# Scores over all 64 rows of a half, with zeros in the unused rows, and the right-hand pools 32 bytes lower

## The chip, the cores and the metric

The kernel runs on one core of a Trainium2 chip. The metric is the device time of one execution in microseconds (us). Before the change three runs gave 1689.62, 1690.02 and 1690.09 us; their median is 1690.02 us.

## The reference

Two mixers of the same 2048 x 512 input (batch 1) are blended by a gate. Everything is float32.

```python
g = sigmoid((x * gate_w).sum(-1, keepdims=True))
# A: Fourier mixing, as matrix products
a = einsum("bsd,ed->bse", x, dft_hid_re);  b = einsum("bsd,ed->bse", x, dft_hid_im)
y = einsum("ts,bse->bte", dft_seq_re, a) - einsum("ts,bse->bte", dft_seq_im, b)
# B: softmax attention, 32 heads of width 16, all 2048 keys for all 2048 queries
q, k, v = split(x @ wqkv)
p = softmax(einsum("bhqd,bhkd->bhqk", q, k) * 16 ** -0.5)
o = einsum("bhqk,bhkd->bhqd", p, v) @ wo
out = g * y + (1 - g) * o
```

The attention weights are drawn 64 times larger than usual, so that the softmax needs a maximum taken off its scores.

## The kernel before

**Precision.** Float32 operands are split into a high and a low part (`hi_lo`, lines 83 to 85: ScalarE copies the high part, VectorE or GpSimd subtracts), and a product is made of three matmuls: high by high, high by low, low by high. For queries and keys the three products are stacked along the contraction instead. A *stack* (`qs`, `ks`, lines 198 to 199) is a tile of 128 partitions by 2048 columns for one pair of heads. Head 0 of the pair has partitions 0 to 63 (a *half*), head 1 has partitions 64 to 127. In each half 48 rows hold the three 16-row parts (`load_stacks`, lines 201 to 210), and rows 48 and 49 hold, in `qs`, the negative row maxima in two parts (`m_rows`, lines 239 to 246) and, in `ks`, ones (line 259). Rows 50 to 63 of a half are not used. There are two buffers of each stack, used in turn by the 16 head pairs.

**Stages.** 1. The projections of queries and keys (lines 171 to 193), to about 95 us. 2. The projection of the values: eight row tiles with 128-row matmuls (line 333), then two groups of four tiles (`four`, lines 304 to 327, matmul at line 315) in which two 64-row matmuls, one in each half of the array, run side by side. `four` also runs the first maxima between its matmuls. 3. The imaginary hidden transform, also with `four`. 4. The main part from about 195 us to about 1,640 us: attention for 16 head pairs, woven with the Fourier transforms. 5. The last output projections.

**The main part.** `segment` (line 888) issues slots from a written pattern such as `FULL`. In a slot a matmul of the transforms (`d`, line 416, 64 rows) goes to one half of the array, and a score (`s`, line 721, 50 rows) or a tile for the row maxima (`a`, line 222, 48 rows) goes to the other half. ScalarE takes the exponential of each score tile from PSUM into `pt` (line 722); VectorE takes the maximum of each `a` tile (line 224). At the bar of a pattern the products with the values (line 757) run: they read `pt` and use all 128 rows. Seven PSUM banks are handed out by a small model of when their readers are done (`bank`, `read_by`); a matmul that gets a bank waits for the reader of its last contents.

**The order around the change.** `st1` is a pool on the right side of the on-chip memory; it holds the tile name `hl` with two buffers. The first `hl` tile is `ones`. Its eight DMAs into `ks`, on GpSimd's queue (line 259), wait until the memory of the first stage is free. The first 12 stack loads (lines 209 and 210) and the four loads of `wo` (line 261 with `staged`, line 104) go through SyncE's queue. Then PE computes the values; `v_done` (line 274) copies half of each result with ScalarE (line 277) and half with VectorE (line 278). At row tiles 6, 8, 10 and 12 `v_done` also splits one quarter of `wo` into a new `hl` tile, so ScalarE gets a cast (line 84) at that place of its queue. A new `hl` tile has to wait for whatever still reads the buffer it takes. In the kernel before, tile 6 takes the second buffer, which nobody has used; tile 8 takes the buffer of `ones`. The value tiles go through four PSUM banks in turn, so tile 11 needs the bank of tile 7.

In the built program the right-hand tiles begin at a multiple of 64 bytes plus 32; `pt`, for example, begins at byte 172,448 of each partition. `xab`, `vt`, `qs`, `ks` and the split weights `wv`, `wre`, `ch`, `cl` are on the left, at multiples of 64.

Of the kernel before, what the change touches and what calls it, by code (L numbers as in the profile page):

```python
# [9 lines left out]
F32 = mybir.dt.float32  # L10
# [5 lines left out]
P = 128  # L16
S = 2048
D = 512
# [13 lines left out]
def mix_kernel(ctx: ExitStack, tc: tile.TileContext, xa_t, xa, wqkv, w_hid, w_seq, wo, gate_w, out):  # L32
# [5 lines left out]
    nc = tc.nc  # L38
# [54 lines left out]
    st1 = right.__enter__()  # L93
# [8 lines left out]
    def staged(src):  # L102
        raw = st1.tile([P, D], F32, name="raw", bufs=RAW)
        nc.sync.dma_start(raw, src)
        return raw
# [92 lines left out]
    qs = [main.tile([P, S], F32R, name=f"qs{i}", tag=f"qs{i}") for i in range(2)]  # L198
    ks = [main.tile([P, S], F32R, name=f"ks{i}", tag=f"ks{i}") for i in range(2)]

    def load_stacks(p):
        q_t, k_t = qs[p % 2], ks[p % 2]
        for h in range(2):
            rows = slice((2 * p + h) * DH, (2 * p + h + 1) * DH)
            o = 64 * h

            for i, (qv, kv) in enumerate(((0, 0), (0, 1), (1, 0))):
                part = slice(o + 16 * i, o + 16 * i + 16)
                nc.sync.dma_start(q_t[part].bitcast(F32), qk_d[0][qv, rows])
                nc.sync.dma_start(k_t[part].bitcast(F32), qk_d[1][kv, rows])  # L210
# [41 lines left out]

    ones = st1.tile([2, 2 * D], F32, name="hl", bufs=2)
    nc.gpsimd.memset(ones, 1.0)
    nc.gpsimd.memset(vt[:, :, :, 16:17], 1.0)
    for i in range(2):
        for h in range(2):
            for tb in range(2):
                nc.gpsimd.dma_start(ks[i][64 * h + 48:64 * h + 50, tb * 2 * D:(tb + 1) * 2 * D].bitcast(F32), ones)
    load_stacks(0)  # L260
    wos = [staged(wo[:, kt]) for kt in range(KT)]
    wrs = []
# [87 lines left out]
    work = ctx.enter_context(tc.tile_pool(name="work", bufs=1, side="right", reuse_waits="tile"))  # L350
# [30 lines left out]
    def bank(i=None):  # L381

        nonlocal now
        if i is None:
            i = min(range(7), key=lambda j: free[j])
        now = max(now, free[i] + 0.7)
        return i, banks[i].tile([P, 512], F32, name="t")

    def read_by(i, kind):

        nonlocal dve, act
        if kind == "a":
            dve = max(now + 2.0, dve) + 2.6
            free[i] = dve + 0.4
        else:
            act = max(now + 2.0, act) + 2.1
            free[i] = act + 0.5
# [7 lines left out]
    class Chain:  # L405


        def __init__(self, take, n):
            self.take, self.left = take, n
            self.begun = False  # L410
# [226 lines left out]
    class LastPair:  # L637


        def __init__(self, blk, acc):  # L640
            self.blk, self.acc = blk, acc
            self.oe = work.tile([P, 512], F32, name="oe", bufs=2)
            self.on = work.tile([P, 4, 2, DH], F32, name="on15", bufs=2)
            self.rc = work.tile([P, 4, 2], F32, name="rc15", bufs=2)
            self.o15 = work.tile([P, 2, P], F32R, name="o15", bufs=2)

        def copy(self, n):
            for c in range(n):
                cols = slice(c * 512 // n, (c + 1) * 512 // n)
                nc.scalar.copy(self.oe[:, cols], self.acc[:, cols])  # L650
# [56 lines left out]
    def scores(u, qb, h, ps=None):  # L707
        p, r = divmod(u, 32)
        hf, kt = divmod(r, 16)
        q0 = hf * 1024 + qb * 512  # L710
        if u >= UNITS - 16:

            blk, kt = divmod(kt, 8)
            q0, kt = 1024 + blk * 512, 2 * kt + qb
        if u not in pts:
            pts[u] = work.tile([P, 4, 512], F32, name="pt", bufs=4)
        if ps is None:
            i, ps = bank()
            read_by(i, "s")
        rr = slice(64 * h, 64 * h + 50)  # L720
        nc.tensor.matmul(ps, ks[p % 2][rr, kt * P:(kt + 1) * P], qs[p % 2][rr, q0:q0 + 512], start=True, stop=True)  # L721
        return nc.scalar.activation(pts[u][:, 2 * qb + h], ps, AF.Exp, bias=0.0, scale=DH ** -0.5)  # L722

# [144 lines left out]
    def score(kind, h):  # L868
        x = next(streams[h][kind == "a"], None)
        if x:  # L870
            if kind == "a":
                i, ps = bank()
                read_by(i, "a")
                users.append((kind, a_tile(*x, ps)))
            else:
                users.append((kind, scores(*x)))
# [65 lines left out]
    def first_tiles(phase, j):  # L942

        if j == 3:
            return scores(*next(streams[0][0]), turn_of("a"))
        a_tile(*next(streams[0][1]))
# [17 lines left out]
    for u in range(valued + 2, UNITS, 2):  # L964
        add_sums()
        run_plan(u)
        for i in range(4):
            if i == 2:
                pump(*whole[u])
                if u == 506:  # L970
                    last_pairs[0].turn()
                elif u == 508:
                    last_pairs[0].back()
            for h in range(2):
                scores(u + i // 2, i % 2, h)
            for h in range(2):
                score("a", h)
        if u == 510:
            last_pairs[0].products(())
        values()  # L980
        if deferred:
            deferred.pop(0)()
# [39 lines left out]
```

## Time and profile before

| | us |
|---|---|
| median of three runs | 1690.02 |
| profiled execution, its own time | 1689.9 |
| its span | 1688.1 |
| PE busy | 1676.5 |
| DVE busy | 1371.2 |
| ACT busy | 1246.1 |
| POOL busy | 747.3 |

PE is TensorE's matmuls, PEld its weight loads, DVE VectorE, ACT ScalarE, POOL GpSimd, and SP (SyncE) issues most DMAs. An engine's name with a q is its instruction queue. A row of groups gives line, engine, operation, output<-inputs by the program's names, shapes, count, busy time, mean duration and the idle time before. A row of the timeline gives the start in us from the span's start, the duration, the engine, what it does, and in brackets how long the engine was idle before and what ended that. The ends of matmuls are modelled, so the distance between the starts of two matmuls says more than their durations.

### The profile page before, as it was taken

To read this page: it belongs to the slowest core of one execution; us is meant where nothing else is said; L and a number is where in the kernel's file an instruction comes from. 1 tells how busy PE (TensorE), PEld (TensorE's weight loads), DVE (VectorE), ACT (ScalarE), POOL (GpSimd) and SP (SyncE) were. 2 spreads that over 40 slices of the span, in tenths; PEclk is the share of its full clock that TensorE was granted. 3 is DMA by queue.
4 is the path that set the end of the run, shared out by engine and by line. 5 is a ranking of instruction groups with operands and counts; after the bars stand their busy time and mean duration, and the time that the engine had idled before them with its cause. 6 is when DMAs were issued, how large, how long until landed. Compare 5 with 4: busy or idle time off the path is not lost.

```text
span 1688.1 us, 34488 instructions
## 1 busy us (share of the span) xinstructions
PE 1676.5 (99%) x13072; PEld 1089.9 (65%) x13072; DVE 1371.2 (81%) x2283; ACT 1246.1 (74%) x2472; POOL 747.3 (44%) x807
## 2 busy tenths in 40 slices
PE   9999999999999999999999999999999999999998
PEld 7888766666666666666666666666666666665643
DVE  5448688888888888888888888888888888899944
ACT  5212288887777888777777788778777888787896
POOL 0214634554444465444444466445554465322230
PEclk9999999999999999999999999999999999999999
DMA  9963500314141533314155543332241536640114
GB/s 289 345 153 112 175 11 20 45 51 77 45 83 46 96 102 84 70 46 95 45 133 189 103 121 85 86 67 61 70 89 46 112 94 131 263 70 8 32 29 139
DMA packets 82485, 165.15 MB, mean 98 GB/s; under 512 B 19776, under 2 KB 20032, under 8 KB 78480
## 3 DMA queue, kind: packets, MB, share of 16 engines
q1 hardware_dynamic: 77968, 162.56, 37.1%
q8 instruction: 103, 1.69, 0.4%
q0 software_dynamic: 4352, 0.39, 0.3%
q14 instruction: 62, 0.51, 0.1%
HBM read 107.73 MB, written 54.52 MB: 96 GB/s over the span
## 4 chain that ended last, share of the span: by engine, by line
PE 98%; POOL 1%; issue 0%; DVE 0%; DMA 0%; ACT 0%; DVEq 0%; POOLq 0%; ACTq 0%
PE d L416 40%; PE t L757 27%; PE t L222 10%; PE t L721 9%; PE t L315 4%; PE t L89 2%; PE t L88 2%; PE t L90 2%; PE t L333 1%; PE t L738 1%; PE t L416 0%; PE t L159 0%; POOL hl L292 0%; PE t L675 0%; DMA b<-hl 0%
## 5 line engine op out<-in xcount | busy, mean ns | idle before, releaser
L224 DVE TENSOR_REDUCE mx<-t 128x1 f32<-128x512 f32 x2022 | 1254.3, 684 | 198.7 <-PE t L222 165.4
L722 ACT ACTIVATE pt<-t 128x512 f32<-128x512 f32 x2048 | 1034.6, 631 | 9.5 <-PE t L721 9.3
L721 PE MATMUL t<-qs,ks 50*128 50x512 f32 x2048 | 740.2, 413 | 0.5 <-ACT y L432 0.5
L222 PE MATMUL t<-ks,qs 48*128 48x512 f32 x2022 | 689.8, 400 | 0.0
L416 PE MATMUL d<-xab,ch 64*128 64x512 f32 x2016 | 644.8, 394 | 0.0
L757 PE MATMUL t<-pt,vt 128*32 128x512 f32 x3968 | 477.5, 598 | 0.0
L416 PEld LDWEIGHTS d<-xab,ch 64*128 64x128 f32 x2016 | 366.7, 184 | 133.3 <-issue 92.2
L222 PEld LDWEIGHTS t<-ks,qs 48*128 48x128 f32 x2022 | 366.5, 186 | 62.4 <-DVE mx L224 27.4
L416 PE MATMUL d<-xab,cl 64*128 64x512 f32 x1008 | 397.9, 395 | 0.0
L721 PEld LDWEIGHTS t<-qs,ks 50*128 50x128 f32 x2048 | 366.9, 185 | 33.5 <-ACT pt L722 13.1
L772 POOL TENSOR_TENSOR osum<-osum,oe 128x512 f32<-128x512 f32 x217 | 279.8, 1290 | 168.2 <-ACT oe L766 161.0
L766 ACT COPY oe<-t 128x512 f32<-128x512 f32 x217 | 127.7, 589 | 238.0 <-PE t L757 235.6
L757 PEld LDWEIGHTS t<-pt,vt 128*32 128x32 f32 x3968 | 105.0, 109 | 227.8 <-issue 148.8
L371 POOL CAST ch<-craw 128x512 fp32r<-128x512 f32 x126 | 77.4, 614 | 347.7 <-PE t L721 278.8
L416 PEld LDWEIGHTS d<-xab,cl 64*128 64x128 f32 x1008 | 185.6, 184 | 68.2 <-issue 51.1
L372 POOL TENSOR_TENSOR cl<-craw,ch 128x512 fp32r<-128x512 f32 x126 | 162.3, 1288 | 10.2
L245 POOL DMA_DIRECT2D qs<-mt x128 | 72.3, 570 | 82.5 <-DVE mt L241 75.9
L416 PE MATMUL d<-wo_hl,o_hl 64*128 64x512 f32 (+1 forms) x270 | 72.6, 393 | 0.8 <-DVE yp_qs L596 0.8
L416 PE MATMUL d<-wre,xab 64*128 64x512 f32 x288 | 70.4, 389 | 0.0
L416 PEld LDWEIGHTS d<-wre,xab 64*128 64x128 f32 x288 | 52.9, 185 | 3.9 <-DVE mx L224 0.3
L416 PEld LDWEIGHTS d<-wo_hl,o_hl 64*128 64x128 f32 (+1 forms) x270 | 49.6, 185 | 4.6 <-DVE yp_qs L596 1.3
L89 PE MATMUL t<-xab,wh 128*128 128x512 f32 x128 | 50.2, 392 | 0.0
(121 smaller groups left out, 895.6 us busy)
## 6 DMA issues: line engine op xcount, KB each, us to landing
craw<-w_seq SPq DMA_DIRECT2D x128, 256.0 KB
qk<-hl SPq DMA_DIRECT2D x32, 512.0 KB
qs<-qk SPq DMA_DIRECT2D x96, 128.0 KB
ks<-qk SPq DMA_DIRECT2D x96, 128.0 KB
b<-hl SPq DMA_DIRECT2D x16, 512.0 KB
xab<-b SPq DMA_DIRECT2D x16, 512.0 KB
o<-osum SPq DMA_DIRECT2D x62, 128.0 KB
oh<-nh SPq DMA_DIRECT2D x12, 512.0 KB
```

What stands on the lines that cost most here:

```text
L89: nc.tensor.matmul(ps, sh, ml, start=False, stop=False)
L222: nc.tensor.matmul(ps, qs[p % 2][r, qt * P:(qt + 1) * P], ks[p % 2][r, kb * 512:(kb + 1) * 512], start=True, stop=True)
L224: user = nc.vector.tensor_reduce(mx[p % 2][:, h, qt, kb:kb + 1], ps, AX.X, ALU.max)
L245: (nc.sync, nc.gpsimd)[h].dma_start(rows.rearrange("v (q b c) -> v b q c", q=8, b=4)[:, b], mt[hf][32 * b + h:32 * b + 32:2])
L371: nc.gpsimd.tensor_copy(h1, raw)
L372: nc.gpsimd.tensor_tensor(l1, raw, h1.bitcast(F32), ALU.subtract)
L416: i = nc.tensor.matmul(self.ps, st[r], mv[r], start=not self.begun, stop=stop)
L721: nc.tensor.matmul(ps, ks[p % 2][rr, kt * P:(kt + 1) * P], qs[p % 2][rr, q0:q0 + 512], start=True, stop=True)
L722: return nc.scalar.activation(pts[u][:, 2 * qb + h], ps, AF.Exp, bias=0.0, scale=DH ** -0.5)
L757: nc.tensor.matmul(acc[32 * j:32 * j + 32], vt[:, kt, p, h:h + 32], pt[:, j], start=u == us[0], stop=u == us[-1])
L766: nc.scalar.copy(oe, acc)
L772: nc.gpsimd.tensor_tensor(o, o, oe, ALU.add)
```

## The change

A second `hl` tile, `zeros`, of 14 partitions by 1024 columns is set to zero by GpSimd. Sixteen more DMAs on GpSimd's queue copy it into rows 50 to 63 of each half of both `ks` and both `qs` buffers; they stand between the eight DMAs of the ones. `zeros` takes the second buffer of `hl`, so the split of `wo` at row tile 6 takes the buffer of `ones`, and the one at row tile 8 that of `zeros`. The score matmul reads 64 rows of each operand where it read 50. The added terms are zero times zero. The matmuls of the maxima keep their 48 rows.

A `pad` tile of 8 float32 columns is allocated in each of the two right-hand pools and never written or read. It puts the tiles of these pools 32 bytes lower; they then begin at multiples of 64 bytes (`pt` at 172,416).

The order of the instructions on PE, DVE, ACT and SP is the same as before. On POOL there are one memset and 16 DMAs more. GpSimd's DMAs use eight semaphores in turn, so with 24 in a row each from the ninth on waits for the landing of the one eight places before. The cast of `wo` at row tile 6 on ScalarE waits for the last of the DMAs of the ones, which is now the 22nd of 24; in the kernel before it waited for no such DMA.

```diff
     ones = st1.tile([2, 2 * D], F32, name="hl", bufs=2)
     nc.gpsimd.memset(ones, 1.0)
+    zeros = st1.tile([14, 2 * D], F32, name="hl", bufs=2)
+    nc.gpsimd.memset(zeros, 0.0)
     nc.gpsimd.memset(vt[:, :, :, 16:17], 1.0)
     for i in range(2):
         for h in range(2):
             for tb in range(2):
                 nc.gpsimd.dma_start(ks[i][64 * h + 48:64 * h + 50, tb * 2 * D:(tb + 1) * 2 * D].bitcast(F32), ones)
+                for t in (ks[i], qs[i]):
+                    nc.gpsimd.dma_start(t[64 * h + 50:64 * h + 64, tb * 2 * D:(tb + 1) * 2 * D].bitcast(F32), zeros)
+    st1.tile([P, 8], F32, name="pad")
     load_stacks(0)
...
             self.o15 = work.tile([P, 2, P], F32R, name="o15", bufs=2)
+            if not blk:
+                work.tile([P, 8], F32, name="pad")
...
-        rr = slice(64 * h, 64 * h + 50)
+        rr = slice(64 * h, 64 * h + 64)
         nc.tensor.matmul(ps, ks[p % 2][rr, kt * P:(kt + 1) * P], qs[p % 2][rr, q0:q0 + 512], start=True, stop=True)
```

## The prediction

> **What bounds the kernel now.** I read the page first, then the timeline of the first 130 us and of one segment of the main part, then the single lines that the change touches. The page:
>
> ```profile
> span 1688.1 us, 34488 instructions
> PE 1676.5 (99%) x13072; PEld 1089.9 (65%) x13072; DVE 1371.2 (81%) x2283; ACT 1246.1 (74%) x2472; POOL 747.3 (44%) x807
> PE 98%; POOL 1%; issue 0%; DVE 0%; DMA 0%; ACT 0%; DVEq 0%; POOLq 0%; ACTq 0%
> L224 DVE TENSOR_REDUCE mx<-t 128x1 f32<-128x512 f32 x2022 | 1254.3, 684 | 198.7 <-PE t L222 165.4
> ...
> L721 PE MATMUL t<-qs,ks 50*128 50x512 f32 x2048 | 740.2, 413 | 0.5 <-ACT y L432 0.5
> ```
>
> PE is busy 99% of the span and the chain that ended last is PE for 98% of it. So a pause of PE anywhere is paid in full, and a shorter matmul is gained unless something next to it already waits. The 413 ns of a score look long, but a busy PE is a modelled overlap; distances between starts decide. Here is one segment of the main part:
>
> ```profile
> 703.30 0.50 PE L416 MATMUL d<-xab,ch 64*128 64x512 f32 x1
> ...
> 703.64 0.39 PE L416 MATMUL d<-xab,cl 64*128 64x512 f32 x1
> ...
> 703.65 0.39 PE L222 MATMUL t<-ks,qs 48*128 48x512 f32 x1
> ...
> 704.08 5.00 DVE L224 TENSOR_REDUCE mx<-t 128x1 f32<-128x512 f32 x8 [0.81 <-PE t L222]
> ...
> 705.76 0.40 PE L721 MATMUL t<-qs,ks 50*128 50x512 f32 x1
> 705.76 0.19 PEld L222 LDWEIGHTS t<-ks,qs 48*128 48x128 f32 x1
> ...
> 706.00 0.40 PE L222 MATMUL t<-ks,qs 48*128 48x512 f32 x1
> 706.14 0.18 PEld L721 LDWEIGHTS t<-qs,ks 50*128 50x128 f32 x1
> ...
> 706.74 0.18 PEld L721 LDWEIGHTS t<-qs,ks 50*128 50x128 f32 x1
> 706.84 0.39 PE L416 MATMUL d<-xab,ch 64*128 64x512 f32 x1
> 706.95 0.40 PE L721 MATMUL t<-qs,ks 50*128 50x512 f32 x1
> 707.27 1.92 PE L757 MATMUL t<-pt,vt 128*32 128x512 f32 x16
> ...
> 709.13 0.50 PE L416 MATMUL d<-xab,ch 64*128 64x512 f32 x1
> ```
>
> From the second slot to the sixteenth are 14 steps. The half with the 64-row transforms takes 706.84 - 703.64 = 3.20 us, 0.2286 a step; the half with scores and maxima 706.95 - 703.65 = 3.30 us, 0.2357 a step. The value products follow the slower half. VectorE is close behind: its eight maxima of the segment start when the first `a` tile is done, and one takes (5.00 - 0.68) / 7 = 0.617 us (0.68 being the duration of one, 684 ns in the groups). The third ends near 705.99 and the fourth near 706.61. A weight load normally starts with the matmul before it on its half (705.76 and 705.76); those at 706.14 and 706.74 start late, each 0.13 to 0.15 us after a maximum should be done. So near the segment's end the scores wait for VectorE to free a bank.
>
> **Part 1: 64 rows instead of 50.** 2048 matmuls and 2048 weight loads change their rows; none is added. One bound is no gain at all: 48 and 50 rows go at one pace here, so a row more or less need not count. The other is that each score falls to the transforms' pace: 0.2357 - 0.2286 = 7.1 ns, times 2048 = 14.5 us. A loss is excluded by the transforms, which have 64 rows and are not slower. I take 1 us of gain. The reason is VectorE: its chain begins with the first `a` of the segment and then runs without a pause, and the late weight loads hang on its third and fourth maxima. Scores that come earlier would wait there; only what lies after that point (about one score a segment) and before the first `a` is left, a few ns in each of some 250 segments.
>
> The Trainium skill, page "TensorE: Matmul & The Clock Gate", section "Part 2: What happens when you issue a matmul", says that the time of a weight load goes by its columns and that the number of rows doesn't matter. By that rule this part gives 0 and the sum below would be 1 us higher; the 7.1 ns between the halves would then be due to waits and semaphores, which the scores have and most transforms have not.
>
> **Part 2: 32 bytes lower.** It touches `pt`, `osum`, `oe`, `y` and the staging tiles. Rows with the moving operand on the right (`wch`, off the 64-byte grid before) and on the left (`wv`, on it):
>
> ```profile
> L315 PE MATMUL t<-wch,xab x256: 388/392/399, 141.7 to 193.8; 64*128 64x512 f32 x128
> ...
> L315 PE MATMUL t<-wv,xab x192: 386/390/493, 115.8 to 141.5; 64*128 64x512 f32 x192
> ```
>
> The medians are 392 and 390 ns. If 2 ns were the price of the old place, the value products (16 in a segment, four side by side, so four steps) would gain 4 x 2 x 250 = 2 us; the rest of the traffic is not on the path. Bounds -2 to +2 us; I take 0, since 2 ns lies inside the spread of either row.
>
> **Part 3: sixteen more DMAs on GpSimd's queue.** This is where I expect the time to change. The place, before:
>
> ```profile
> 100.21 4.31 POOL L259 DMA_DIRECT2D ks<-hl  x8 [5.49 <-DMA qk<-hl]
> ...
> 106.06 5.06 SPq L104 DMA_DIRECT2D raw<-wo  x4
> ...
> 115.75 1.20 PE L315 MATMUL t<-wv,xab 64*128 64x512 f32 x8
> 115.99 0.62 ACT L84 CAST hl<-raw 128x512 fp32r<-128x512 f32 x1 [2.46 <-DMA raw<-wo]
> 116.52 0.38 ACT L277 COPY vt<-t 128x256 f32<-128x256 f32 x1
> ...
> 116.80 0.39 PE L222 MATMUL t<-ks,qs 48*128 48x512 f32 x2
> ...
> 116.94 0.42 DVE L278 COPY vt<-t 128x256 f32<-128x256 f32 x1 [2.94 <-ACT vt L277]
> ...
> 118.40 1.77 PE L315 MATMUL t<-wv,xab 64*128 64x512 f32 x14
> ```
>
> The cast at 115.99 is the split of `wo` at row tile 6. After the change it waits for the 22nd of the 24 DMAs. Queued behind it on ScalarE is the copy of value tile 7 (116.52), behind that VectorE's half (ends 117.36), and behind VectorE's copy the maxima. PE needs tile 7's bank when `four` starts its second phase. Of the last row's 14 matmuls six belong to the first phase, so that start is 118.40 + 3 x 0.23 = 119.09 (a step of the row being (1.77 - 0.39) / 6 = 0.23). The slack is 119.09 - 117.36 = 1.7 us. From the cast's start to the end of VectorE's copy are 1.37 us.
>
> When does the 22nd land?
>
> ```profile
> L259 POOL DMA_DIRECT2D ks<-hl x8: 521/521/689, 100.2 to 104.0; - x8
> ...
> DMA to landing us min/median/max: 5.2/8.9/11.3
> ```
> ```profile
> qs<-mt POOLq DMA_DIRECT2D x128, 2.0 KB, 1.7
> ```
> ```profile
> 95.00:116.00 21.00, 21.00 (x94) 17.14 (x95) 3.99 (x10) 2.70 (x8) 4.31 (x8) 1.00 0.91 149
> 116.00:130.00 14.00, 14.00 (x124) 11.43 (x124) 11.35 (x20) 3.19 (x8) 2.62 (x3) 1.00 0.28 100
> ```
>
> The eight issues are 0.54 us apart (100.2 to 104.0). The first lands 5.2 us after its issue, at 105.4, the last 11.3 us after, at 115.3: one each 1.41 us, because the DMA engines are 91% busy with the stack loads until 116. Early bound: at the pace of the issue, with the 1.7 us of a quiet GpSimd DMA, number 22 lands at 100.2 + 21 x 0.54 + 1.7 = 113.2, ahead of 115.99, and nothing is lost. Late bound: at 1.41 us each, 105.4 + 21 x 1.41 = 135.0. Between them: each new DMA brings 14 rows of 4 KB, 57 KB, together 0.92 MB; at the 149 GB/s of that stretch they take 6.2 us, so that the busy time which ended at 116 ends some 4 us later, near 120, when 105.4 + 10 x 1.41 = 119.5 has seen eleven landings. The other eleven go at the pace of the issue: 119.5 + 11 x 0.54 = 125.4. I take that; it lies halfway between the ends, and each end needs one of the two paces to hold throughout.
>
> The cast then starts at 125.5, VectorE's copy ends at 126.9, and PE's second phase starts 126.9 - 119.09 = 7.8 us late. The stack loads, slowed by the same DMAs, hold up the first maxima tile (116.80) for some of that time; it is the same pause, not another. GpSimd itself waits longer between its issues (from the ninth on for a landing), but its next work is the subtraction behind the same cast.
>
> **Part 4: the clock.** PE would stand still for several us, which it does nowhere in the trace between its first and last matmul.
>
> ```profile
> 2.17 3.78 PE L159 MATMUL t<-wch 128*128 128x512 f32 x8 [2.17 <-DVE wch L156]
> 5.75 0.71 PE L88 MATMUL t<-xab,wh 128*128 128x512 f32 x1
> ...
> 7.73 0.40 PE L89 MATMUL t<-xab,wh 128*128 128x512 f32 x1
> ```
> ```profile
> 1679.81 1.01 PE L675 MATMUL t<-w,o 32*128 32x512 f32 x12
> ```
> ```profile
> 1682.00:1689.00 7.00, 0.00 (x0) 0.00 (x0) 0.91 (x2) 0.00 (x0) 0.84 (x1) 0.61 0.42 162
> ```
>
> The first eight matmuls are (5.75 - 2.17) / 8 = 0.45 us apart, twice the later 0.23, and the pace is full from 7.73. After the last matmul (ends 1680.8) the granted clock of the last 7 us is 0.61, as if it fell to one half at 1683.5, 2.7 us after. So a pause of 5 us may cost up to (7.7 - 2.2) / 2 = 2.8 us more, or nothing; I take the middle, 1.4.
>
> The Trainium skill, page "TensorE: Matmul & The Clock Gate", section "Part 1: The HAM clock gate", says that an idle window of about 3.4 us halves the clock, and a busy one of that length restores it. By that rule the term would be an estimated 3.4 / 2 = 1.7 us, 0.3 more than the middle of the rows. The rows at both ends of this trace agree with it.
>
> **The sum.** + 7.8 (PE's pause) + 1.4 (clock) - 1.0 (scores) + 0 (addresses) = + 8.2 us. The profiled execution took 1689.9 us (a span of 1688.1 and 1.8 around it), 0.1 from the median 1690.02. 1690.0 + 8.2 = 1698.2 us.
>
> **The rivals.** *The DMAs land in time.* If number 22 lands before 117.7, the slack hides it and no clock is lost: 1690.0 - 1.0 = 1689.0. For it speaks the quiet DMA of 1.7 us, against it the 8.9 us that even two rows took in this place. Chance 0.14, with pauses up to 3 us counted here.
>
> *The rows are what slows the scores* (the other side). Then the gain is up to 14.5 us, and with the pause 1690.0 + 9.2 - 14.5 = 1684.7. It decides once a score gains over 4.5 ns, if VectorE doesn't hold it. For it speaks the difference between the halves; against it that 48 and 50 rows cost the same, and the late weight loads. Chance 0.11.
>
> *The slow pace holds to the end*: number 22 lands at 135.0, the cast is 19 us late, PE 17.4 us, the clock costs 2.8: 1690.0 + 17.4 + 2.8 - 1.0 = 1709.2. For it speaks that each landing here waited for large loads; against it that those loads end. Chance 0.13.
>
> **How the numbers follow.** My forecast of 1694 to 1703 has 0.62. No change means within 0.2%, 3.4 us, about what a measurement of this kernel can tell. Faster: the rows' rival, 0.11. Same: the DMAs in time and a little of the forecast's lower edge, 0.16. Slower: the rest, 0.73. The range that leaves out most of the rows' rival and the worst of the slow pace is 1687 to 1709.
>
> **What would show it.** In the profile after: the landings of line 261 and 263 reach to about 127; the first cast of `wo` on ScalarE starts near 125.5, released by a DMA of `hl` into the stacks and not by `raw<-wo`; PE shows its first gap of several us between 116 and 127, and slow matmuls behind it; from then on everything is shifted and a segment still takes 5.83 us from one first transform to the next (703.30 to 709.13 here). I am wrong if that gap is missing, if it is twice as long, or if segments are shorter by more than 0.02 us, which would mean that rows or addresses count.

## The result, and the profile after

The changed kernel takes 1698.26 us (median of five runs, 1697.54 to 1699.17) against 1690.02 (five runs, 1689.61 to 1690.18): a ratio of 1.0049, 95% interval 1.0034 to 1.0064, or 8.2 us slower. The profiled execution took 1698.26 us with a span of 1696.5. The page after:

```profile
span 1696.5 us, 34516 instructions
...
PE 1679.3 (99%) x13072; PEld 1090.6 (64%) x13072; DVE 1370.1 (81%) x2283; ACT 1245.9 (73%) x2472; POOL 755.8 (45%) x824
...
q0 software_dynamic: 4864, 1.31, 0.6%
...
PE 96%; DMA 2%; POOL 1%; issue 0%; DVE 0%; ACT 0%; DVEq 0%; ACTq 0%; POOLq 0%
...
L728 PE MATMUL t<-qs,ks 64*128 64x512 f32 x2048 | 740.4, 413 | 0.5 <-ACT y L437 0.5
```

The scores with 64 rows are busy for 740.4 us, 413 ns each; before it was 740.2 and 413. The span is 8.4 us longer, but PE is busy for only 2.8 us more: the rest is time in which PE stands. The chain that ended last has 2% of DMA (0% before), and the row of GpSimd's queue (`q0`: packets, MB, share of the DMA engines) names a small transfer, 1.31 MB (0.39 before). Where it bites is in the timeline of the value projection:

```profile
115.20 1.20 PE L320 MATMUL t<-wv,xab 64*128 64x512 f32 x8
115.62 0.52 POOL L263 DMA_DIRECT2D ks<-hl  x1 [0.23 <-DMA qs<-hl]
116.24 0.40 PE L222 MATMUL t<-ks,qs 48*128 48x512 f32 x2
...
117.84 1.08 PE L320 MATMUL t<-wv,xab 64*128 64x512 f32 x7
...
121.16 0.52 POOL L261 DMA_DIRECT2D ks<-hl  x1 [1.43 <-DMA ks<-hl]
121.86 0.52 POOL L263 DMA_DIRECT2D ks<-hl  x1 [0.19 <-issue]
122.38 0.52 POOL L263 DMA_DIRECT2D qs<-hl  x1
123.19 0.62 ACT L84 CAST hl<-raw 128x512 fp32r<-128x512 f32 x1 [10.21 <-DMA ks<-hl]
123.71 0.37 ACT L282 COPY vt<-t 128x256 f32<-128x256 f32 x1
...
124.12 0.42 DVE L283 COPY vt<-t 128x256 f32<-128x256 f32 x1 [10.68 <-ACT vt L282]
...
124.60 2.07 PE L320 MATMUL t<-wv,xab 64*128 64x512 f32 x7 [5.67 <-DVE vt L283]
126.05 1.05 PE L222 MATMUL t<-ks,qs 48*128 48x512 f32 x2
126.47 2.76 PE L320 MATMUL t<-wv,xab 64*128 64x512 f32 x10
```

The 22nd DMA of the 24, the last one of the ones, is issued at 121.16. It waited 1.43 us for the landing of the DMA eight places before. The cast of `wo` on ScalarE starts at 123.19; it has been idle for 10.21 us, released by a DMA of `hl` into `ks`, where before it was `raw<-wo` and 2.46 us. Behind it come ScalarE's copy (123.71), VectorE's copy (124.12), and PE, which had been idle for 5.67 us. Its next seven matmuls of this line cover 2.07 us, where eight of them covered 1.20 at 115.20. The windows (columns: stretch, its length, busy time of PE, PEld, DVE, ACT and POOL with counts, the granted clock, the DMA share, GB/s) show the clock:

```profile
95.00:116.00 21.00, 21.00 (x96) 17.15 (x96) 3.43 (x9) 2.70 (x7) 8.82 (x17) 1.00 0.92 152
116.00:130.00 14.00, 8.33 (x53) 6.62 (x51) 4.71 (x9) 0.90 (x2) 5.01 (x9) 0.76 0.50 125
...
6.45:122.45 116.00, 112.47 (x508) 92.80 (x508) 48.49 (x93) 38.08 (x69) 24.77 (x35) 1.00 0.93 276
122.50:129.25 6.75, 4.65 (x22) 3.67 (x24) 4.01 (x7) 0.90 (x2) 1.66 (x2) 0.50 0.45 135
129.35:1692.55 1563.20, 1557.79 (x12535) 991.17 (x12533) 1315.44 (x2179) 1204.24 (x2398) 728.60 (x782) 1.00 0.34 84
```

In 116 to 130 PE is busy for 8.33 of 14 us (14.00 before). From 122.5 to 129.25 the granted clock is 0.50, on both sides of it 1.00.

How much each part took, I read from the starts of the matmuls, the n-th of one trace beside the n-th of the other. Up to the pause the kernel after is 0.56 us ahead, because the full clock came at 6.42 us and not at 7.58. The first two matmuls behind the pause, one in each half of the array, come 6.05 and 5.83 us later than that lead would have them: a pause of 5.9. When the clock is full again both halves together are 8.2 us late: so the slow clock cost 2.3. From there to the end the difference (with the lead in it) goes from 7.66 to 8.34, but the same comparison of the versions below, which all have the pads, drifts by anything from - 0.29 (the seventh experiment) to + 1.09 (the sixth), with the pause and without it. So no part of the drift can be put down to the change.

One segment of the main part, after:

```profile
710.90 0.50 PE L421 MATMUL d<-xab,ch 64*128 64x512 f32 x1
710.90 0.50 PE L728 MATMUL t<-qs,ks 64*128 64x512 f32 x1
...
711.24 0.39 PE L421 MATMUL d<-xab,cl 64*128 64x512 f32 x1
711.24 0.39 PE L222 MATMUL t<-ks,qs 48*128 48x512 f32 x1
...
714.44 0.39 PE L421 MATMUL d<-xab,ch 64*128 64x512 f32 x1
714.53 0.39 PE L728 MATMUL t<-qs,ks 64*128 64x512 f32 x1
...
716.70 0.50 PE L421 MATMUL d<-xab,ch 64*128 64x512 f32 x1
```

The transforms' half takes 714.44 - 711.24 = 3.20 us from the second slot to the sixteenth, the scores' half 3.29; before it was 3.20 and 3.30. This one segment is 5.80 us long (5.83 before), but no segment is typical to 0.03 us: where two full segments follow each other, the mean from one first transform to the next is 5.82 us before and after. Over the 192 full segments of each trace the mean from the first slot to the sixteenth is 3.54 us in the transforms' half and 3.64 us in the scores' half, before and after alike.

### The profile page after: what moved, and what is told of

Read it like the earlier page. It is cut to its first block, busy times and chain, and to the rows that moved or that the text cites. A ratio compares the mean times of both kernels' runs of the same rounds, so it can differ in the third digit from the quotient of the medians.

```text
span 1696.5 us, 34516 instructions
## 1 busy us (share of the span) xinstructions
PE 1679.3 (99%) x13072; PEld 1090.6 (64%) x13072; DVE 1370.1 (81%) x2283; ACT 1245.9 (73%) x2472; POOL 755.8 (45%) x824
## 3 DMA queue, kind: packets, MB, share of 16 engines
q0 software_dynamic: 4864, 1.31, 0.6%
## 4 chain that ended last, share of the span: by engine, by line
PE 96%; DMA 2%; POOL 1%; issue 0%; DVE 0%; ACT 0%; DVEq 0%; ACTq 0%; POOLq 0%
PE d L421 40%; PE t L764 27%; PE t L222 10%; PE t L728 9%; PE t L320 4%; PE t L89 2%; PE t L88 2%; PE t L90 2%; PE t L745 1%; DMA ks<-hl 1%; DMA qs<-hl 1%; PE t L421 0%; PE d L222 0%; DMA qk<-hl 0%; PE t L159 0%
## 5 line engine op out<-in xcount | busy, mean ns | idle before, releaser
L728 PE MATMUL t<-qs,ks 64*128 64x512 f32 x2048 | 740.4, 413 | 0.5 <-ACT y L437 0.5
L222 PEld LDWEIGHTS t<-ks,qs 48*128 48x128 f32 x2022 | 371.0, 186 | 62.2 <-DVE mx L224 27.2
L728 PEld LDWEIGHTS t<-qs,ks 64*128 64x128 f32 x2048 | 366.9, 185 | 34.0 <-ACT pt L729 14.1
L320 PE MATMUL t<-wch,xab 64*128 64x512 f32 x256 | 51.5, 391 | 0.0
```

The costliest lines, as they stand in the source:

```text
L222: nc.tensor.matmul(ps, qs[p % 2][r, qt * P:(qt + 1) * P], ks[p % 2][r, kb * 512:(kb + 1) * 512], start=True, stop=True)
L320: i = nc.tensor.matmul(ps[c], st[r], mv[r], start=phase < 2 and j == 0, stop=phase > 1 and j == 11)
```

## The experiments

The theory: the cast of `wo` waits for the last DMA that reads the buffer of the ones, PE stands for that long, and its clock then costs some more; rows and addresses count for nothing. The rivals: the extra DMA traffic itself delays something (a split load, the stacks), or the rows or the addresses take a part. The experiments start from the kernel after, unless said otherwise.

**The ones first.** The 24 DMAs stay, but the eight of the ones lead; the cast then waits for the eighth.

```diff
                 nc.gpsimd.dma_start(ks[i][64 * h + 48:64 * h + 50, tb * 2 * D:(tb + 1) * 2 * D].bitcast(F32), ones)
+    for i in range(2):
+        for h in range(2):
+            for tb in range(2):
                 for t in (ks[i], qs[i]):
```

> The changed kernel with one difference: the eight DMAs of the ones are issued first, then the sixteen of the zeros. All bytes, rows and addresses stay. Theory of the wait: ScalarE's cast of wo at row tile 6 then waits only for the eighth GpSimd DMA, which lands near 115.5 us, so PE's pause of 5.7 us and the slow clock behind it go: 1690.0 us, at most 1 us more (slack 1.7 us). Rival, the traffic itself: 0.92 MB more in a stretch where the DMA engines are over 90% busy delay the loads of wo and the stacks whatever waits for what: the cast starts after 119 us and the time stays at 1695 us or more.

Measured: 1689.88 us, ratio 1.0001 (0.9992 to 1.001). Its timeline and its windows:

```profile
116.68 0.62 ACT L84 CAST hl<-raw 128x512 fp32r<-128x512 f32 x1 [3.74 <-DMA raw<-wo]
...
117.62 0.42 DVE L286 COPY vt<-t 128x256 f32<-128x256 f32 x1 [4.21 <-ACT vt L285]
...
123.18 0.52 POOL L266 DMA_DIRECT2D qs<-hl  x1
```
```profile
116.00:130.00 14.00, 14.00 (x124) 12.23 (x122) 11.39 (x21) 3.40 (x8) 7.30 (x11) 1.00 0.70 168
```

The cast waits for the load of `wo` again. GpSimd's last DMA is issued at 123.18, even later than in the kernel after, and in 116 to 130 the DMA engines are busier (0.70 against 0.50). PE doesn't stand. So all of the 8.2 us hang on the place of the ones in the queue and none on the traffic by itself. This version has the 64 rows, the zeros and the pads too, and equals the kernel before, within a gain of 1.4 and a loss of 1.7 us: they give nothing that these runs can see.

**A tile of its own for the zeros.** The order of the DMAs stays mixed, but tile 6 finds the second buffer of `hl` unused.

```diff
-    zeros = st1.tile([14, 2 * D], F32, name="hl", bufs=2)
+    zeros = st1.tile([14, 2 * D], F32, name="zeros")
```

> The changed kernel with one difference: the zeros have a tile name of their own and not the second buffer of hl, so the 24 DMAs stay interleaved as they are, but the cast at row tile 6 gets a buffer that nobody reads. Theory of the wait: 1690.0 us, at most 1 us more; the cast starts at about 116 us, released by the load of wo; the cast at row tile 8 waits for the ones instead, which have landed. Rival, the traffic itself: 1695 us or more.

Measured: 1689.97 us, ratio 1.0001 (0.9991 to 1.001). The cast and the windows of 116 to 130:

```profile
115.68 0.62 ACT L84 CAST hl<-raw 128x512 fp32r<-128x512 f32 x1 [2.60 <-DMA raw<-wo]
```
```profile
116.00:130.00 14.00, 14.00 (x126) 11.43 (x124) 11.70 (x21) 3.03 (x8) 6.37 (x10) 1.00 0.58 151
```

The load of `wo` releases the cast, and PE is busy throughout, at full clock, with the DMAs in the very order of the kernel after. It is the sharing of the buffer that costs.

**The scores on 50 rows**, with everything else as after.

```diff
-        rr = slice(64 * h, 64 * h + 64)
+        rr = slice(64 * h, 64 * h + 50)
```

> The changed kernel with all its DMAs and pads, but the scores read 50 rows again. Theory that the rows count for nothing: 1698.3 us, within 0.7 us. Rival, that 64 rows gain something that the pause hides: slower than the changed kernel, by up to 14.5 us if a score gained the whole 7.1 ns. Second rival, that 64 rows cost something (between the stages the changed kernel falls behind by another 0.8 us from 210 to 1680 us): 1697.5 us.

Measured: 1698.61 us, ratio 1.0052 (1.0039 to 1.0065): as after, within the interval. The timeline has the same pause:

```profile
123.43 0.62 ACT L84 CAST hl<-raw 128x512 fp32r<-128x512 f32 x1 [9.79 <-DMA ks<-hl]
...
124.84 2.07 PE L320 MATMUL t<-wv,xab 64*128 64x512 f32 x7 [5.25 <-DVE vt L283]
```

**The pads alone**, on the kernel before.

```diff
+    st1.tile([P, 8], F32, name="pad")
...
+            if not blk:
+                work.tile([P, 8], F32, name="pad")
```

> The kernel before with the two pads alone: all right-hand tiles 32 bytes lower, nothing else. Theory that addresses count for nothing: 1690.0 us, within 0.5 us. Rival: 2 ns for each step of the value products and of the matmuls that stream a right-hand tile, 1688 us. Second rival, that the other 0.8 us of the changed kernel come from the addresses: 1690.8 us.

Measured: 1690.2 us, ratio 1.0004 (0.9995 to 1.0012). The 32 bytes are worth between a gain of 0.8 and a loss of 2.0 us, with no change in between: nothing that these runs can see. The rival's gain of 2 us is ruled out; a loss of 0.8 us, the second rival, is not.

**A warm pause.** PE runs 22 matmuls whose results nobody uses ahead of the second phase of the first `four`, where it stands otherwise.

```diff
+            if phase == 1 and done is v_done and ss[0] == 8:
+                for _ in range(22):
+                    nc.tensor.matmul(ps[2], ab[8][:, 0, :P], wv[0][0], start=True, stop=True)
```

> The changed kernel with 22 matmuls of 128 rows put between the first and second phase of the first four value tiles, into a PSUM bank that the second phase clears; their results are not used. They take 22 x 0.227 = 5.0 us and stand where PE pauses for 5.7 us. Theory that the pause costs twice, once by standing and once by the clock: the wait for ScalarE's cast stays, the granted clock stays full, and the 2.0 us that the slow clock cost behind the pause go: 1696.3 us. Rival, that the steps behind the pause are slow because VectorE has to catch up with its maxima: the clock is full and the time stays at 1698.3 us or grows.

Measured: 1696.3 us, ratio 1.0038 (1.0023 to 1.0052). The timeline and the windows:

```profile
119.13 5.30 PE L317 MATMUL t<-wv,xab 128*128 128x512 f32 x22
...
123.52 0.62 ACT L84 CAST hl<-raw 128x512 fp32r<-128x512 f32 x1 [10.08 <-DMA ks<-hl]
...
124.36 1.77 PE L323 MATMUL t<-wv,xab 64*128 64x512 f32 x8
```
```profile
116.00:130.00 14.00, 13.93 (x90) 10.54 (x88) 5.22 (x10) 0.90 (x2) 4.89 (x8) 1.00 0.52 125
```

The cast is as late as after, but the clock stays at 1.00. Against before this version loses 6.5 us and the kernel after 8.2; the difference of the medians, 1.7 us, is what the slow clock costs. The rival has a small part: once the 22 are left out of the count, the first matmuls of both halves are 5.8 us late (5.9 after), and some 0.6 us more are lost behind them at full clock, where weight loads wait for VectorE's maxima (0.41 us at 126.13, 0.25 at 128.52). From then on they are 6.4 us late for good.

**Each DMA of the zeros twice**, so that the last of the ones is the 36th of 40.

```diff
-                for t in (ks[i], qs[i]):
+                for t in (ks[i], qs[i], ks[i], qs[i]):
```

> The changed kernel with each of the sixteen DMAs of the zeros issued twice, 40 on GpSimd's queue in all; the last of the ones is the 36th. Theory of the wait: fourteen more landings before it, each between 0.52 us (the pace of the issue) and 0.87 us (the mean pace of the changed kernel, 105 to 123 us), so the cast starts at 130.5 to 135.4 us where it started at 123.2, and the time is 1698.3 + 7.3 to 12.2 = 1705.6 to 1710.5 us; the clock costs no more than it did. Rival, that the wait is for the loads and not for the ones: 1699 us or less.

Measured: 1718.76 us, ratio 1.0172 (1.0156 to 1.0187): 29 us slower, far above what was expected. The timeline:

```profile
118.63 0.52 POOL L263 DMA_DIRECT2D ks<-hl  x1 [8.23 <-DMA ks<-hl]
119.14 0.52 POOL L263 DMA_DIRECT2D qs<-hl  x1
119.65 0.52 POOL L261 DMA_DIRECT2D ks<-hl  x1
120.16 0.52 POOL L263 DMA_DIRECT2D ks<-hl  x1
120.67 0.52 POOL L263 DMA_DIRECT2D qs<-hl  x1
122.70 0.52 POOL L263 DMA_DIRECT2D ks<-hl  x1 [1.51 <-DMA ks<-hl]
...
140.80 0.52 POOL L261 DMA_DIRECT2D ks<-hl  x1
...
143.18 0.62 ACT L84 CAST hl<-raw 128x512 fp32r<-128x512 f32 x1 [30.26 <-DMA ks<-hl]
...
144.59 2.07 PE L320 MATMUL t<-wv,xab 64*128 64x512 f32 x7 [25.72 <-DVE vt L283]
```

The direction is as the theory has it: the cast waits for a DMA into `ks`, PE for the cast. The size is not, and the fault lies in the experiment. The second DMA of a pair writes the rows of the first and so waits for its landing. That is the row with the wait in each group of five: `ks` at 120.16, its twin at 122.70, after a wait of 1.51 us. Five DMAs take some 4.2 us that way (122.70 to 126.91 for the next such row). A wait of my own was added beside the one that I meant to lengthen; the run confirms the path from the ones to PE, and says nothing on the pace of independent DMAs.

**Zeros into `ks` alone**, scores on 50 rows: 16 DMAs, the last of the ones is the 15th.

```diff
-                for t in (ks[i], qs[i]):
+                for t in (ks[i],):
...
-        rr = slice(64 * h, 64 * h + 64)
+        rr = slice(64 * h, 64 * h + 50)
```

> The changed kernel with the zeros put into the key stacks alone, 16 DMAs in all on GpSimd's queue, and the scores reading 50 rows (rows 50 to 63 are left out of them). The last of the ones is the 15th. Theory of the wait: it lands at about 105 + 13 x 0.87 = 116 to 117.5 us, the slack of 1.7 us behind the load of wo (116.0) hides it or nearly: 1690.0 to 1691 us, no gap on PE over 1 us, a full clock. Rival, that a GpSimd DMA costs its share whenever the cast waits for some of them (half of 8.2 us): 1694 us.

Measured: 1693.88 us, ratio 1.0025 (1.0014 to 1.0035). That is the number of the rival, in which each DMA costs a share, and the time alone does not tell it from a wait that I had put too short. The timeline shows the wait:

```profile
120.06 0.62 ACT L84 CAST hl<-raw 128x512 fp32r<-128x512 f32 x1 [6.98 <-DMA ks<-hl]
...
121.47 0.97 PE L320 MATMUL t<-wv,xab 64*128 64x512 f32 x6 [2.44 <-DVE vt L283]
```
```profile
119.25:122.65 3.40, 1.18 (x8) 0.68 (x8) 1.66 (x4) 0.90 (x2) 1.27 (x1) 1.00 0.01 2
122.75:126.05 3.30, 3.30 (x16) 2.64 (x18) 2.64 (x5) 0.00 (x0) 0.00 (x0) 0.50 0.71 238
126.15:132.00 5.85, 5.85 (x54) 4.84 (x53) 4.50 (x9) 1.18 (x3) 0.94 (x1) 1.00 0.02 4
```

The trace has the 15th landing at 119.88, some 3 us later than I had put it: the DMAs issued from 108 to 115 all landed between 117.7 and 120.2, as the large loads came to an end. Behind the pause the matmuls are 2.7 us late, and 4.7 once the clock is full again. So a pause of 2.44 us costs 2.0 us more, and 1.7 of that is the clock (half of the 3.41 us at half clock). That is the second half of the miss, since I had expected a short pause to be free of it.

Left open: why the half with scores and maxima steps every 234 ns and the transforms' half every 227 (medians of starts in the 192 full segments, with 50 rows and with 64). The rows of the scores are ruled out; waits and semaphores are what the prediction named beside them, and no run tried those.

## Why the prediction was right

The time was forecast at 1698.2 us and came out at 1698.26. The mechanism held: a wait of PE for the last DMA of the ones, and a slow clock behind it. The agreement to 0.1 us is luck, because three terms were off and their errors cancel: the pause by - 1.9 us, the clock by + 0.9, the scores by + 1.0.

- **PE's pause, + 7.8: too large; 5.9 measured.** The chain was as told, from the cast's start to PE's next matmul too (124.60 - 123.19 = 1.41 us; 1.37 forecast). The landing of the 22nd was mis-sized: 122.86 instead of 125.4, or 2.0 us early if the 0.56 us by which this whole execution was ahead is added. The slow pace was right: the first nine landings came 1.34 us apart (104.65 to 115.34; 1.41 forecast). So was, roughly, the longer busy time: from 116 to 119 the DMA engines are 0.92 busy, 0.20 before, and from 119 to 122 they are at 0.38. That is some 3 us more where I had put 4, without saying why 4 and not the 6.2 of the bytes. Wrong was the end: thirteen had landed by 118.93, where I had eleven at 119.5, and the others did not go at the pace of the issue. They had been issued already, up to eight at a time, and seven of them landed between 121.59 and 122.57, 0.16 us apart. The 22nd itself was issued at 121.16, after the 14th had landed (120.88), and landed 1.70 us later.
- **The clock, + 1.4: 2.3 in the trace after, 1.7 by the medians with and without the warm pause.** The two differ by some 0.6 us that PE waits for VectorE behind the warm pause; in the kernel after no weight load shows such a wait there. The price depends on the pause's place against the clock's windows (below), so that it differs from run to run: 2.9 us in the trace with 50 rows, 2.0 with the half of the zeros. The estimate of 3.4 / 2 = 1.7 by the Trainium skill (page "TensorE: Matmul & The Clock Gate", section "Part 1: The HAM clock gate") came nearer than the middle of my rows.
- **The scores, - 1.0: nothing.** The pace is the same with 50 and 64 rows. The 7.1 ns between the halves were never a price of rows, so the reason I gave, that VectorE would hold back what the scores gain, was not put to the test: there was no gain to hold. The other sentence of the Trainium skill that I had cited (page "TensorE: Matmul & The Clock Gate", section "Part 2: What happens when you issue a matmul") agrees: the weight load of a score takes 185 ns with 50 and with 64 rows.
- **The addresses, 0: not contradicted.** The pads alone show no change, within a gain of 0.8 and a loss of 2.0 us.
- **The first maxima tile, said to be held up: wrong.** It starts at 116.24, before at 116.80; the difference is the lead of 0.56. It cost nothing in the sum, since I had counted it as the same pause.

5.9 + 2.3 = 8.2 us, as the forecast's 7.8 + 1.4 - 1.0. In this pair of traces the lead (- 0.56) and the drift (+ 0.68) about cancel. Of the signs named beforehand, the releaser, the place of the gap and the slow matmuls were as told; the cast starts at 123.19, not 125.5, and landings reach to 124.7, not 127. The limit of 0.02 us for a segment was too narrow for a single one, as the 5.80 above shows; the mean is unchanged. The rivals fall: the 22nd landed 5 us too late for the slack, rows gave nothing, and the slow pace ended with the large loads.

## What to carry to other kernels

A scratch tile that takes a buffer from a rotating pool hands its readers on to whoever takes that buffer next: before adding one, see which later tile gets it, what is queued behind that tile's first write, and which DMA is the last reader. Here the same work in another order, or with a tile of its own, costs nothing. Count such a DMA's landing by the traffic around it and by the landings that its own issue waits for, not by its size. To a pause of PE add some 2 us for the clock; here even one of 2.4 us cost that.

## What the runs showed of the hardware that I had not expected

**The clock is decided in fixed windows.** In the traces with a pause the full clock lasts 116.05 us from its first grant to its loss, in all four alike (kernel after, 50 rows, zeros twice, half of the zeros), though the pauses begin at the same work and the grant comes at 6.0 to 8.0 us. The half clock then lasts 6.83, 6.83, 27.31 and 3.41 us: two, two, eight and one times 3.41. The 116.05 are 34 times 3.413, and the 1563.3 to the next loss are 458 times. The place of these windows against the kernel differs between executions, and with it the first grant (from 5.2 to 8.0 us over nine traces). The Trainium skill, page "TensorE: Matmul & The Clock Gate", section "Part 1: The HAM clock gate", states such a free-running window of 3413 ns, and the traces agree. It also says, under "HAM oscillation", that gaps over about 3.4 us are the ones to avoid; here the run with half of the zeros lost the clock after 2.44 us. Its window from 119.25 to 122.65 shows PE busy for 1.18 of 3.40 us. With 50 rows a window with more work left the clock at full:

```profile
117.20:120.55 3.35, 2.39 (x21) 1.62 (x17) 0.00 (x0) 0.00 (x0) 1.98 (x4) 1.00 0.75 141
120.65:123.95 3.30, 0.00 (x0) 0.00 (x0) 0.00 (x0) 0.52 (x1) 1.54 (x3) 1.00 0.40 71
```

So the loss came with 35% of a window busy and not with 71%. The ends of the traces, where PE runs out of work, narrow this, if the smaller matmuls there count alike. In the trace before, the window that ends with the loss at 1683.53 has PE busy for 0.70 of 3.41 us (21%), with the pads alone for 1.28 (38%); with the ones first, a window with 1.97 (58%, from 1678.44) left the clock at full. The prediction let the end of the trace before agree with an idle window of 3.4 us; the clock fell 2.7 us after the last matmul, and what fits is a window that was idle for the most part. The way back takes more: with 50 rows a window with 76% busy (from 124.01) did not bring the full clock back, and the next, busy throughout, did.

**Small DMAs beside large ones.** The sources of the kernel after give the time from issue to landing (least, median, most):

```profile
L263 POOL DMA_DIRECT2D ks<-hl x8: 518/518/560, 100.4 to 121.9; - x8
...
DMA to landing us min/median/max: 2.2/7.0/11.1
```

A DMA of 14 rows of 4 KB takes 2.2 us at the least and 7.0 in the median. In the quiet of the run with the zeros twice the median of the same DMAs is 2.3. The Trainium skill, page "DMA: Bandwidth & Descriptors", section "Anatomy of one DMA — SWDGE (gpsimd) path", gives a fit of 2.0 us plus the bytes over 436 thousand bytes a microsecond, an estimated 2.1 us for these 57 KB. That is near the 2.3 measured in the quiet, and under a third of the 7.0 beside the large loads.
